# A redrawn order table, five x tiles and four transposed ones, fillers ahead of early waits, and fewer last stores in a fused attention and routed MLP kernel

## The chip, the cores and the metric

The kernel runs on one core of one Trainium2 chip. The metric is the device time of one execution in microseconds; the median of three runs of the kernel before is 752.19 us (751.41 to 753.65). A core has TensorE (PE; PEld is its loading of weights, which overlaps), VectorE (DVE), ScalarE (ACT), GpSimd (POOL) and SyncE (SP, which here only issues transfers), each with its own queue of instructions in program order; they wait for one another by semaphores.

## What is computed

```python
# x: B=8, H=8, S=512, D=64     state: B=8, H=8, Ns=32, D=64
scores = scale * x @ state.T;   a = softmax(scores);    xread = a @ state
scores2 = scale * state @ x.T;  a2 = softmax(scores2);  sread = a2 @ x
t = concat([xread, sread], axis=2)      # 544 tokens per b, laid out as 4352 x 512

logits = t @ w_gate                     # 512 x 8 experts
P = exp(logits - logits.max())
for _ in range(8):                      # Sinkhorn
    P /= P.sum(1, keepdims=True) + 1e-9
    P /= P.sum(0, keepdims=True) + 1e-9
    P *= N / E
out = sum over e of P[:, e:e+1] * (relu(t @ w1[e]) @ w2[e])     # w1[e] 512x1024, w2[e] 1024x512
```

Every token goes through every expert; P only weighs the results.

## The kernel before

The work has two stages. The first holds the attention, the gate, the Sinkhorn loop and expert 0, all mixed; the second holds experts 1 to 7, one block of tokens after the other. There are nine blocks: eight of 512 x tokens (one per b) and one of 256 state tokens (all b together).

The first stage is a list of operations. Each has a number, the engines it may run on, the operations it comes after, and the tiles it takes. `PLAN` is a table written out by hand: each entry is an operation number and a letter for its engine (P TensorE, V VectorE, A ScalarE, G GpSimd, S SyncE's queue, H nothing on the chip). `issue` walks through the table and emits each operation on its engine; so the table sets the order on every engine and, where an operation may run on several, which one runs it. Numbers such as `{"DVE": (0.60, 0.80)}` and the due times beside them are a planner's costs; the emitted code does not read them. Tiles of a pool are handed out in turn (`Ring`, `Slot`): the next one waits until the readers of the tile that had the same place are through.

For each b, the parts of the first stage are:

- two loads of x (`x_nat`, line 468), issued on GpSimd's queue, into one of four tiles of pool `axp`;
- transposed x (`xT`), one of three tiles of pool `axt`: for b 0 and 1 by TensorE (line 578) and copies (`keepX`), for the rest by DMA transposes that SyncE issues (line 591);
- for each half q of the heads, scores on TensorE (`psB`, line 605), and for the first two half-groups also direct scores (`psA`, line 684) that need the spread state `stD`;
- softmax A (x attends to the state): transpose to `eA` (line 628), row maximum (`mxA`, 631), subtraction (`subA`, 648), exponential on ScalarE (656), sums and reciprocals (666, 667), normalization (`normA`, 670, on VectorE or GpSimd), transpose to `aT` (674; for the first two half-groups by TensorE, line 709, and a copy);
- softmax B (the state attends to x): maximum `nmB` (640), bias `nsB` (644), exponential `E` (652), reciprocal `rrec` (659), normalization (`normB`, 662, on VectorE or GpSimd), a DMA transpose to `ETs` that SyncE issues (line 742), and the read `su_ps` (line 758), kept in `xsT` by `keepS`.

The state itself is loaded into `st_st`, cast to `st_in`, transposed by TensorE (line 492) and kept as `stT`. `G_ps` (line 520) is the gate's weight seen through the state; `gate_ps` (788) gives the logits. The Sinkhorn loop (lines 826 to 848) alternates VectorE work with a TensorE matmul by ones (`csb_ps`, line 846) that sums over partitions.

Expert 0: `v_ps` (line 870) projects w1 through the state into `V` (read out by ScalarE or VectorE), `hps` (line 897) is the hidden layer, `hT` its relu, `yps` (line 935) the second layer, kept in `acc`. At the end of the table come expert 1's first projections and hidden block, its sums of weights `T` (`sums_w`, line 965), and then the second stage.

In the second stage `layer2` (line 324 on) forms a block's second product from seven products of 128x256 matmuls (line 334) that accumulate in the banks A, E and two banks `Bseed`; `layer1` (line 255) makes the next block's hidden layer between them, and `project` (line 235) the next projections. Where n is 0, at the very first block, `seed` (line 353) opens each `Bseed` bank with one matmul whose result is overwritten, and `weigh` multiplies expert 0's result by P. `layer2_last` handles the state tokens of the last expert: two rows of 128 tokens, the second in two column halves, each row stored by four transfers of 32 tokens (line 317), two on SyncE's and two on ScalarE's queue.

Of the kernel before, what the change touches and what calls it, by code (L numbers as in the profile page):

```python
# [17 lines left out]
46V 62P 50H 51G 61A 71V 63P 60A 52G 64V 11G 72V 73A 80P 65V 12G 435P 401P 66A 81V 13H 79P 14G 82V 436A 88V  # L18
437A 404P 83A 67V 402A 137H 403A 89V 96H 97P 100P 84V 406A 68V 90A 98A 15G 85V 69P 86P 53G 405A 99V 87V 70A
103P 101A 102A 91V 409P 16H 92G 413P 104V 407P 410A 411P 105V 111A 438P 120P 414V 408A 419P 421P 106V 415P  # L20
112V 138S 121V 74V 439A 412A 422V 113V 417P 107A 54G 440A 75G 122V 432P 429P 123V 370V 420A 469P 128A 418A
416A 17G 108V 140P 124A 125V 423P 426P 471A 433P 114A 148V 93S 129V 430P 149V 172H 424P 76S 434A 115V 470A
109G 130V 139S 110V 126G 141V 131A 427P 18G 127V 142V 428V 431A 445P 143V 132V 94P 150A 95V 77P 425A 156P 116G
447P 151V 133V 78V 449P 446A 443P 441P 144A 455P 164V 152G 448A 117S 19H 450V 157V 444A 165V 173S 442A 451P
456A 166A 134S 20G 452A 453P 463P 158V 472P 207H 145V 175P 159V 183V 184V 457P 31G 146G 454A 176V 473A 160A
464P 185A 174S 460P 458P 461P 465A 147V 161V 21G 153S 177V 191P 47P 162G 474A 118P 167V 459A 154P 462A 178V
163V 135P 49A 168G 199V 22H 48V 179A 466P 136A 352P 475P 200V 192V 201A 193V 119V 467P 476A 194V 23G 195A 485P
202V 208S 210P 180V 169S 155A 218V 356P 353A 481P 357V 468A 487P 219V 24G 489P 181G 186V 211V 242H 486A 482A
477P 490V 488A 483P 479P 220A 170P 478A 503P 187G 480A 484V 171A 203G 196V 537P 209S 25H 212V 226P 197G 504A
505A 506P 213V 500P 182V 198V 26G 234V 221V 507A 222V 204S 188S 491P 27G 538A 227V 539A 501P 497P 502A 508A  # L30
492P 235V 243S 228V 244S 214A 229V 511P 215V 236A 523P 230A 498P 494P 216G 245P 495P 515P 512V 499A 277H 231V
524A 493A 517P 246V 253V 223S 496A 247V 521P 516A 237V 254V 519P 509P 522V 518A 248V 513P 232G 189P 520A 255A
205P 510V 224P 514V 540P 28H 278S 261P 249A 190V 269V 29G 225A 270V 262V 531P 534P 206V 238G 250V 532P 256V
358P 271A 535P 217V 541A 533A 233V 542A 312H 279S 263V 272V 536A 354P 280P 528P 543P 529P 525P 288V 289V 251G
555P 264V 281V 265A 282V 239S 257V 526P 359A 266V 544A 530V 556A 545P 355A 547P 549P 273G 553P 527A 546V 571P
313S 290A 548A 283V 605P 550A 554V 296P 267G 606V 304V 572A 305V 240P 573A 557P 284A 607A 558A 551P 297V 552A
568P 360P 258S 241V 285V 30G 291V 306A 559P 562P 574P 298V 252V 315P 299V 286V 569P 576A 268V 323V 563P 575A
274S 300A 560P 570A 292G 316V 361A 561A 581P 564A 307V 565P 362P 324V 317V 301V 325A 302G 566P 363V 582A 326V
579P 587P 583P 287V 314S 588V 591P 567A 580A 639P 608P 584A 592A 347H 303V 331P 577P 348G 641V 640A 610A 609A
339V 293S 589P 585P 275P 332V 259P 578A 327G 586A 260A 590A 294P 340V 308G 333V 341A 593P 309S 318V 319A 334V  # L40
295V 364P 594P 276V 328S 625P 619P 342V 595A 335A 365A 599P 320V 602P 343V 336V 600P 337V 603P 626A 321G 322V
329P 310P 350G 344S 601A 349G 311A 620V 345P 338V 346V 604V 366P 596P 330A 368P 369V 351G 597P 367A 371V 611P
372P 598A 695H 615P 617P 373V 612V 374P 375V 613P 614V 616A 623P 618A 621P 696H 711H 376A 705P 377V 642P 624A
622A 706A 707A 630P 643V 697V 708P 644A 378P 379V 631P 710A 627P 698V 380V 647P 632A 709A 636P 628P 381P 633P
699V 648V 637P 382V 634P 657P 629A 638A 383V 700V 653P 658A 655P 384P 651P 635A 701V 654A 725P 385V 723P 386V
702V 656A 726A 716P 652A 724A 717A 645P 659P 649P 714P 646A 650A 660A 387P 721P 715A 712P 727P 687P 722A 388V
728A 688A 667P 713A 664P 389V 390P 703V 665P 668P 391V 673P 674A 392V 661P 670P 669A 729V 393P 671P 394V 666A
662P 672A 677P 395V 718P 663A 678A 679P 675P 683P 719A 681P 720V 680A 676A 685P 396P 684A 682A 397V 686A 692P
704V 689P 693P 690P 730P 398V 694A 399P 733P 731V 691A 732A 735A 734A 400V
# [68 lines left out]
def kernel(  # L118
# [63 lines left out]
    outs = out.rearrange("(b s) d -> b s d", s=SB)[:, S:, :]  # L182
# [32 lines left out]
    axp = actx.enter_context(tc.tile_pool(name="attn_x", bufs=4))  # L215
    axt = actx.enter_context(tc.tile_pool(name="attn_xt", bufs=3))
# [46 lines left out]
    def layer1(e, bi):  # L263
# [35 lines left out]
    def layer2_last():  # L299
# [4 lines left out]
        nb = 128 // Ns  # L304
        for row in range(tn // 128):
# [10 lines left out]
            for i in range(nb):  # L316
                (nc.scalar if i % 2 else nc.sync).dma_start(
                    out=outs[row * nb + i], in_=acc[ds(i * Ns, Ns), k, :])

    def layer2(e, bi, n):  # L320
# [30 lines left out]
        def seed(i):  # L351
            bb = bank([128, 2, DH], FP32, "Bseed", "B%d" % i)
            nc.tensor.matmul(bb.rearrange("p c d -> p (c d)"), identh, aT[:, 0, 0], start=True, stop=True)
# [12 lines left out]
        if not n:  # L366
            seed(1)
# [67 lines left out]
    st_in = spl.tile([128, B, NQ, 2, D], FP16, name="st_in")  # L435
    st_st = spl.tile([128, B, NQ, D], FP32, name="st_st")
    loads = []
    for g in range(2):
        def load(g=g):
            bs = ds(g * B // 2, B // 2)  # L440
            (nc.scalar if g else nc.sync).dma_start(
                out=st_st[:, bs], in_=state[bs].rearrange("b (q h) n d -> (h n) b q d", q=NQ))

        loads.append(dma((0, 0), 1.0, load, lands=2.7))
        ops[-1].since, ops[-1].hard = 0.5, 1
# [14 lines left out]
    xn = [slot(axp, 4, [128, H, NSC * D], FP16, "x_nat") for _ in range(B)]  # L460
# [649 lines left out]
```

## Time and profile before

| | us |
|---|---|
| median of three runs | 752.19 |
| the profiled execution | 752.75 |
| its span, first to last instruction | 751.0 |
| TensorE busy | 736.0 |
| VectorE busy | 617.0 |
| ScalarE busy | 517.7 |
| GpSimd busy | 70.8 |

In the span's 40 slices a digit is the busy share in tenths. In a row of stages the columns are the stretch, its length, and then each engine's busy time with its number of instructions, the granted TensorE clock (1.00 is full), the share of the DMA engines and GB/s. In a row of the timeline the first number is the start, the second the length of a run of equal instructions; the bracket gives the idle time ahead of it on its engine and what ended it. In a row of groups stand line, engine, operation, written and read tile, shapes and count, then busy us and mean ns of one, then the idle time before. The end of a matmul is modelled, so two neighbours overlap in the rows; the step from start to start is the better measure of what one costs.

### The profile page before, as it was taken

What the parts mean: (1) busy time and instruction counts of PE and PEld (TensorE: products, weight loads), DVE (VectorE), ACT (ScalarE), POOL (GpSimd) and SP (SyncE); (2) the same over time, 40 slices, a digit from 0 to 9 for tenths busy, and PEclk for the clock granted to TensorE, in tenths of its full rate; (3) what the DMA queues carried; (4) which work ended last, traced back from release to release, by engine and by line L of the source; (5) the groups of instructions that cost most, each with busy time, mean ns of one, the idle gap of its engine ahead of it and who ended that gap; (6) DMA issues with size and microseconds to landing.
All of it is one profiled execution on the core that took longest, in us unless ns stands there. A gap on an engine that the chain in (4) does not pass through costs nothing.

```text
span 751.0 us, 16151 instructions
## 1 busy us (share of the span) xinstructions
PE 736.0 (98%) x6517; PEld 502.2 (67%) x6517; DVE 617.0 (82%) x1529; ACT 517.7 (69%) x1014; POOL 70.8 (9%) x81
## 2 busy tenths in 40 slices
PE   5999999999999999999999999999999999999997
PEld 3444445666777777776776767776777767767776
DVE  5899989877888789788888788887897888887885
ACT  6876856799876766667666766667666676667662
POOL 4674410200010000100000000100001000000000
PEclk9899999999999999999999999999999999999999
DMA  9997560600033000700007000330007000002234
GB/s 179 140 134 131 82 99 1 109 6 1 1 61 53 2 1 2 113 1 2 1 2 112 2 1 1 58 57 1 1 2 112 2 1 2 1 31 94 103 113 141
DMA packets 51323, 36.71 MB, mean 49 GB/s; under 512 B 25392, under 2 KB 43824, under 8 KB 51248
## 3 DMA queue, kind: packets, MB, share of 16 engines
q0 software_dynamic: 22272, 20.97, 18.5%
q1 hardware_dynamic: 27744, 14.18, 7.6%
q8 instruction: 51, 0.84, 0.5%
q10 hardware_dynamic: 1232, 0.52, 0.3%
q14 instruction: 24, 0.20, 0.1%
HBM read 42.48 MB, written 8.91 MB: 68 GB/s over the span
## 4 chain that ended last, share of the span: by engine, by line
PE 92%; DVE 3%; DMA 1%; ACT 1%; POOL 1%; issue 0%; SPq 0%; POOLq 0%; DVEq 0%; ACTq 0%
PE hps L255 28%; PE Bseed L334 20%; PE A L334 14%; PE E L334 14%; PE yps L935 6%; PE hps L897 4%; PE v_ps L235 4%; DMA xT<-x_nat 1%; DMA x_nat<-in_x_dram 1%; PE y L312 0%; PE v_ps L870 0%; POOL a L670 0%; ACT Hm L275 0%; DVE acc L348 0%; POOL E L662 0%; PE su_ps L758 0%
## 5 line engine op out<-in xcount | busy, mean ns | idle before, releaser
L275 ACT ACTIVATE Hm<-hps 128x512 f16<-128x512 f32 (+1 forms) x496 | 265.8, 577 | 130.5 <-PE hps L255 128.1
L255 PE MATMUL hps<-aT,V 128*128 128x512 f16 x880 | 230.6, 379 | 0.0
L334 PEld LDWEIGHTS <-Hm 128*128 128x128 f16 x1888 | 181.6, 98 | 71.3 <-issue 15.9
L348 DVE SCALAR_TENSOR_TENSOR acc<-Bseed,Pmat,acc 128x256 f32<-128x256 f32 x354 | 155.0, 477 | 9.8 <-PE Bseed L334 6.9
L334 PEld LDWEIGHTS <-sm 128*128 128x128 f16 x1416 | 138.3, 98 | 34.5 <-issue 0.3
L334 PE MATMUL A<-w2h,Hm 128*128 128x256 f16 x944 | 123.7, 273 | 0.0
L334 PE MATMUL Bseed<-T,Hm 128*128 128x256 f16 x944 | 123.3, 273 | 0.0
L255 PEld LDWEIGHTS <-V 128*128 128x128 f16 x880 | 86.1, 98 | 50.8
L348 DVE SCALAR_TENSOR_TENSOR acc<-E,Pmat,acc 128x256 f32<-128x256 f32 x236 | 103.2, 476 | 13.8 <-PE E L334 13.5
L281 DVE TENSOR_TENSOR sm<-Hm 128x512 f16<-128x512 f16 (+1 forms) x122 | 50.1, 411 | 60.4 <-ACT Hm L275 60.2
L243 ACT CAST V<-v_ps 128x512 f16<-128x512 f32 x144 | 74.2, 612 | 0.0
L348 DVE SCALAR_TENSOR_TENSOR acc<-A,Pmat,acc 128x256 f32<-128x256 f32 x118 | 51.9, 479 | 17.9 <-PE A L334 17.6
L935 PE MATMUL yps<-w2h,hT 128*128 128x512 f16 x272 | 64.1, 379 | 0.1
L334 PE MATMUL E<-w2h,sm 128*128 128x256 f16 x472 | 61.7, 273 | 0.0
L334 PE MATMUL E<-T,sm 128*128 128x256 f16 x472 | 61.6, 273 | 0.0
L334 PE MATMUL Bseed<-T,sm 128*128 128x256 f16 x472 | 61.5, 272 | 0.0
L363 ACT COPY Bseed<-A 128x512 f32<-128x512 f32 (+1 forms) x62 | 34.1, 550 | 37.9 <-PE A L334 35.3
L282 DVE TENSOR_TENSOR Hm<-Hm 128x512 f16<-128x512 f16 (+1 forms) x122 | 50.3, 412 | 4.2
L284 DVE TENSOR_TENSOR sm<-Hm,sm 128x512 f16<-128x512 f16 (+1 forms) x122 | 50.2, 412 | 4.2
L283 DVE TENSOR_TENSOR sm<-sm,Hm 128x512 f16<-128x512 f16 (+1 forms) x122 | 49.4, 405 | 0.0
L194 POOL DMA_DIRECT2D w1h<-in_moe_w_dram x12 | 8.5, 714 | 396.9 <-PE hps L255 396.5
L935 PEld LDWEIGHTS <-hT 128*128 128x128 f16 x272 | 25.4, 99 | 28.9 <-issue 1.8
(127 smaller groups left out, 617.7 us busy)
## 6 DMA issues: line engine op xcount, KB each, us to landing
w1h<-in_moe_w_dram POOLq DMA_DIRECT2D x16, 512.0 KB, 7.0
w2h<-in_moe_w_dram POOLq DMA_DIRECT2D x16, 512.0 KB, 8.4
out_dram<-acc SPq DMA_DIRECT2D x32, 256.0 KB, 2.5
x_nat<-in_x_dram POOLq DMA_DIRECT2D x16, 256.0 KB, 5.6
st_st<-in_state_dram ACTq DMA_DIRECT2D x1, 256.0 KB, 4.9
st_st<-in_state_dram SPq DMA_DIRECT2D x1, 256.0 KB, 4.2
ETs<-E SPq DMA_TRANSPOSE x16, 4.3
out_dram<-acc SPq DMA_DIRECT2D x4, 64.0 KB, 1.8
```

Source lines behind the costliest of these rows:

```text
L235: nc.tensor.matmul(ps[q][ds(j * Ns, Ns), :], stT[ds(r, 64), bi, q, ds((j ^ q) * Ns, Ns)], w1h[ds(r, 64), 2 * q + j // 2, cols], tile_posit ...
L243: nc.scalar.copy(out=dst, in_=src)
L255: nc.tensor.matmul(out, lhs, rhs, start=(k == 0), stop=(k == len(terms) - 1))
L275: nc.scalar.activation(out=Hm[:, i, j, :tn], in_=hps[:, :tn], func=AF.Relu)
L281: nc.vector.tensor_add(s1, a21, a22)
L282: nc.vector.tensor_sub(a21, a11, a21)
L283: nc.vector.tensor_sub(s2, s1, a11)
L284: nc.vector.tensor_sub(s4, a12, s2)
L334: nc.tensor.matmul(dst[:, c], lhs(j, c), rhs[:, j], start=first and c == 0 and j == 0, stop=(j == NJ - 1), skip_group_check=True)
L348: nc.vector.scalar_tensor_tensor(out=dst, in0=src[:, c], scalar=p[:, k], in1=dst, op0=ALU.mult, op1=ALU.add)
L363: nc.scalar.copy(out=Bb[:, :nk], in_=A[:, :nk])
L935: nc.tensor.matmul(yps.tile, hT[fb].tile[:, ds(tk * 128, 128)], w2h[:, fb, :], start=(fb == 0), stop=(fb == NFB - 1))
```

## The change

- `PLAN` is written anew: other orders on all engines, and other engines for some operations. It has 784 entries (before 736); the Sinkhorn steps are split into single operations so that other work can stand between them, and the sums of weights become single operations that may run on GpSimd.
- The pool of x has five tiles and that of transposed x four. `st_st` and `st_in` no longer have tiles of their own: they are the first tile of these two pools.
- `IDLE` gives operations ahead of which TensorE gets fillers: matmuls of the identity with itself into the tile that the operation then overwrites. Fifty stand ahead of the first transposes of x (operation 56), three ahead of each of the two direct scores (63, 80), eight ahead of a transpose of the second x (97).
- `subA` may run on GpSimd; on GpSimd `normB` is a tensor-tensor product with a broadcast reciprocal instead of a tensor-scalar one.
- The seeds go: the bank of the first `Bseed` is lent to the first `hps` of the second block, which now stands right after the first A product, ahead of the copy of A. `weigh` is done in another order.
- The state tokens of four b are interleaved in `xsT`, so that a row of 128 tokens can be stored by one transfer. The last two rows are stored by three transfers: one for the first row, and one for each half of the second row as soon as that half is done.

In the instruction lists of both kernels, ahead of the second stage: GpSimd runs 12 subtractions (before 0), 10 `normA` (12), 12 `normB` (12) and 6 sums of weights (0); VectorE runs 2 subtractions from `eA` (14), 6 `normA` (4), 4 `normB` (4), 2 sums of weights (8), 5 copies of `xT` (2), 2 of `aT` (1), 4 of `xsT` (9) and 13 of `hT` (16). Ahead of the first `hps` TensorE runs 40 matmuls of `v_ps` (24) and the 64 of `G_ps` (0). On TensorE 6570 matmuls are issued in all: 64 fillers more and two seeds less than before.

```diff
+IDLE = {56: 50, 63: 3, 80: 3, 97: 8}
...
-def issue(ops):
+def issue(ops, idle):
     for step in PLAN:
...
+        idle(op.takes[0].tile if op.takes else None, IDLE.get(int(step[:-1]), 0))
         op.emit(ENGINES[step[-1]])
...
-    outs = out.rearrange("(b s) d -> b s d", s=SB)[:, S:, :]
+    nb = 128 // Ns
+    outs = out.rearrange("(g b s) d -> g s b d", b=nb, s=SB)[:, S:, :, :]
...
-    axp = actx.enter_context(tc.tile_pool(name="attn_x", bufs=4))
-    axt = actx.enter_context(tc.tile_pool(name="attn_xt", bufs=3))
+    axp = actx.enter_context(tc.tile_pool(name="attn_x", bufs=5))
+    axt = actx.enter_context(tc.tile_pool(name="attn_xt", bufs=4))
...
-                hps = bank([128, S], FP32, "hps", "h")
+                if lent is None:
+                    hps = bank([128, S], FP32, "hps", "h")
+                else:
+                    hps, lent = lent, None
...
-            for i in range(nb):
-                (nc.scalar if i % 2 else nc.sync).dma_start(
-                    out=outs[row * nb + i], in_=acc[ds(i * Ns, Ns), k, :])
+                (nc.scalar if c + 1 < parts else nc.sync).dma_start(
+                    out=outs[row, :, :, cols], in_=acc[:, k, cols])
...
-        def seed(i):
-            bb = bank([128, 2, DH], FP32, "Bseed", "B%d" % i)
-            nc.tensor.matmul(bb.rearrange("p c d -> p (c d)"), identh, aT[:, 0, 0], start=True, stop=True)
-            seeds.append(bb)
-
         if not n:
-            for k, eng in enumerate(("DVE", "ACT", "DVE", "POOL")):
+            for k, eng in ((2, "DVE"), (3, "POOL"), (0, "DVE")):
                 weigh(k, eng)
         product(A, h(0, 0), w2h[:, :NJ, :DH], True)
+        Bb = seeds[n % 2]
         if not n:
-            seed(0)
-        Bb = seeds[n % 2]
+            yield
         nc.scalar.copy(out=Bb[:, :nk], in_=A[:, :nk])
+        if not n:
+            weigh(1, "ACT")
         yield
         product(Eb, s(0), T[:, 0], True)
-        if not n:
-            seed(1)
...
-    st_in = spl.tile([128, B, NQ, 2, D], FP16, name="st_in")
-    st_st = spl.tile([128, B, NQ, D], FP32, name="st_st")
+    early = [Slot(rings.setdefault("xT", Ring(4)),
+                  lambda: axt.tile([128, B, NQ, 2, D], FP16, name="st_in", tag="xT")),
+             Slot(rings.setdefault("x_nat", Ring(5)),
+                  lambda: axp.tile([128, B, NQ, D], FP32, name="st_st", tag="x_nat"))]
...
             def normB(eng, E2=E2, rrec=rrec):
-                engines[eng].tensor_scalar(out=E2.tile, in0=E2.tile, scalar1=rrec.tile, scalar2=None,
-                                           op0=ALU.mult)
+                if eng == "POOL":
+                    nc.gpsimd.tensor_mul(E2.tile, E2.tile, rrec.tile.broadcast_to((128, S)))
+                else:
+                    nc.vector.tensor_scalar(out=E2.tile, in0=E2.tile, scalar1=rrec.tile, scalar2=None, op0=ALU.mult)
...
-                s1 = op(r(4), {"DVE": (0.60, 0.80)}, subA, [m1], [], [eA, mxA])
+                s1 = op(r(4), {"DVE": (0.60, 0.80), "POOL": (1.05, 1.20)}, subA, [m1], [], [eA, mxA])
...
-                copy(eng, xsT[:, ds(2 * q, 2), ds(b * Ns, Ns)], su.tile)
+                copy(eng, xsT.rearrange("p c (g n b) -> p c g n b", g=B // nb, b=nb)[:, ds(2 * q, 2), b // nb, :, b % nb], su.tile)
...
-        nc.vector.tensor_sub(T[:, i, jj], p[:, jj], q[:, jj])
+        engines[eng].tensor_sub(T[:, i, jj], p[:, jj], q[:, jj])
...
+    def idle(t, n):
+        if not n:
+            return
+        t = t.rearrange({2: "p a -> p a", 3: "p a b -> p (a b)", 4: "p a b c -> p (a b c)"}[len(t.shape)])[:, :128]
+        for _ in range(n):
+            if t.dtype == FP16:
+                nc.tensor.transpose(t, identh, identh)
+            else:
+                nc.tensor.matmul(t, identh, identh, start=True, stop=True, skip_group_check=True)
+
+    issue(ops, idle)
...
+        if not i:
+            seeds += [bank([128, 2, DH], FP32, "Bseed", "B%d" % k) for k in range(2)]
         l2 = layer2(e, bi, i)
...
+            l1 = layer1(*work[i + 1], None if i else seeds[0].rearrange("p c d -> p (c d)"))
+        if not i:
+            next(l2)
+            next(l1)
```

More of the change, by code (lines that the diff above doesn't have):

```diff
@@ L22 @@
[L22 to L31, printed above, removed]
@@ L442, in load @@
                 out=st_st[:, bs], in_=state[bs].rearrange("b (q h) n d -> (h n) b q d", q=NQ))
-        loads.append(dma((0, 0), 1.0, load, lands=2.7))
+        loads.append(dma((0, 0), 1.0, load, uses=early[1:], lands=2.7))
         ops[-1].since, ops[-1].hard = 0.5, 1
@@ L459 @@
     makeh.since, makeh.hard = 0.7, 1
-    xn = [slot(axp, 4, [128, H, NSC * D], FP16, "x_nat") for _ in range(B)]
+    xn = [slot(axp, 5, [128, H, NSC * D], FP16, "x_nat") for _ in range(B)]
     x_ready = []
@@ L483, in place @@
                 copy(eng, st_in[:, bs, :, s_, :], st_st[:, bs])
-            bd.append(op((0, 0, g), {"DVE": (0.50, 0.64)} if s_ else {"ACT": (0.50, 0.65)}, place, loads[g:g + 1] + warmed))
+            bd.append(op((0, 0, g), {"DVE": (0.50, 0.64)} if s_ else {"ACT": (0.50, 0.65)}, place, loads[g:g + 1] + warmed, uses=early))
     stT_ready = []
@@ L811 @@
     part("ones")
-    op((30.0,), {"DVE": (0.2, 0.3)}, lambda _: nc.vector.memset(ones128, 1.0))
+    ones = op((30.0,), {"DVE": (0.1, 0.25)}, lambda _: nc.vector.memset(ones128, 1.0))
     part("K")
@@ L820 @@
     gb = psum([128, 1], FP32, "gm_ps")
-    c = sk({"PE": (0.18, 0.45)}, lambda: nc.tensor.matmul(gb.tile, ones128[0:1, :], sm_["gm"]), [c], takes=[gb])
+    c = sk({"PE": (0.18, 0.45)}, lambda: nc.tensor.matmul(gb.tile, ones128[0:1, :], sm_["gm"]), [c, ones], takes=[gb])
     c = sk({"DVE": (0.12, 0.25)}, lambda: nc.vector.tensor_copy(out=tile_of("nm", [128, 1]), in_=gb.tile),
@@ L842, in colnorm, with col_rec, col_mul @@
+        def col_rec():
+            nc.vector.reciprocal(out=sm_["crec"], in_=sm_["crec"])
+        def col_mul():
+            nc.vector.scalar_tensor_tensor(out=Pmat, in0=sm_["crec"].unsqueeze(1).broadcast_to((128, NTB, E)),
                                            scalar=float(N) / float(E), in1=Pmat,
                                            op0=ALU.mult, op1=ALU.mult)
-        c = sk({"DVE": (2.10, 2.25)}, rownorm, [c])
+        for emit, us, tail in ((row_sums, 0.43, 0.03), (row_eps, 0.20, 0.03), (row_rec, 0.37, 0.03),
+                               (row_mul, 0.45, 0.03), (col_part, 0.62, 0.15)):
+            c = sk({"DVE": (us, us + tail)}, emit, [c])
```

127 lines of the change are left out of this document (73 added, 54 removed).

## The prediction

> **What bounds the kernel now.** I read the page's busy shares and slices first, then cut the span into stages where TensorE's work changes, then TensorE's timeline in each stage that is not full.
>
> ```profile
> span 751.0 us, 16151 instructions
> PE 736.0 (98%) x6517; PEld 502.2 (67%) x6517; DVE 617.0 (82%) x1529; ACT 517.7 (69%) x1014; POOL 70.8 (9%) x81
> PE   5999999999999999999999999999999999999997
> ```
>
> TensorE (PE) is busy 98% of the span; only the first and the last slice are not full. The stages (us, PE busy, PEld, DVE, ACT, POOL, granted clock, DMA) say what is lost where:
>
> ```profile
> 0.00:6.86 6.86, 0.01 (x1) 0.01 (x1) 1.53 (x4) 2.72 (x4) 6.11 (x14) 1.00 0.87 144
> 6.86:18.86 12.00, 9.86 (x121) 7.03 (x121) 9.29 (x23) 9.15 (x20) 1.40 (x2) 0.88 1.34 199
> 18.86:22.76 3.90, 3.90 (x16) 1.13 (x23) 3.30 (x7) 2.59 (x5) 2.33 (x2) 0.50 1.23 180
> 22.76:135.14 112.38, 110.59 (x1091) 53.47 (x1076) 102.16 (x245) 80.76 (x179) 41.57 (x39) 1.00 0.62 92
> 135.14:743.35 608.21, 608.03 (x5283) 438.30 (x5276) 498.11 (x1248) 422.48 (x808) 19.35 (x25) 1.00 0.17 34
> 743.35:751.00 7.65, 3.63 (x26) 2.25 (x23) 2.60 (x5) 0.00 (x0) 0.00 (x0) 0.92 0.65 206
> ```
>
> The stage of experts 1 to 7, 608.21 us long, idles 0.18 us: nothing but removed TensorE work can shorten it. What the change can win lies ahead of 135.14 (a start of 6.86 us, a thin stretch, 3.90 us at half clock, 1.79 us of waits) and in the tail. The early rows in time (start, length):
>
> ```profile
> 1.00 0.29 POOL masks.py:199 TENSOR_SCALAR_AFFINE_SELECT identh<-identh 128x128 f16<-128x128 f16 x1
> 6.86 1.03 PE L578 MATMUL xT_ps<-identh,x_nat 128*128 128x128 f16 x8 [6.86 <-DMA x_nat<-in_x_dram]
> 9.39 1.06 PE L578 MATMUL xT_ps<-identh,x_nat 128*128 128x128 f16 x8
> 14.63 0.62 PE L578 MATMUL xT_ps<-identh,x_nat 128*128 128x128 f16 x8
> 18.86 3.57 PE L897 MATMUL hps<-aT,V 128*128 128x512 f16 x8
> 22.36 0.58 PE L870 MATMUL v_ps<-w1h,stT 64*32 64x512 f16 x8
> 22.98 1.90 PE L897 MATMUL hps<-aT,V 128*128 128x512 f16 x8
> 26.54 0.41 PE L870 MATMUL v_ps<-w1h,stT 64*32 64x512 f16 x8
> 26.77 0.29 PE L605 MATMUL psB<-xT,stT 64*32 64x256 f16 x8
> ```
>
> Eight equal matmuls take 3.57 us at 18.86 and 1.90 at 22.98: the first dense work falls into the half-clock stretch. The same eight transposes take 1.03 and 1.06 us early and 0.62 at 14.63, so TensorE is slow at the very start as well.
>
> **The change, part by part.** The sum is made on the profiled execution, 752.75 us (its span is 751.0), which lies 0.56 above the median of the runs, 752.19.
>
> *Start of the dense stretch.* Fifty transposes of the identity go ahead of the first x transpose. The identity is there at 1.29; at the slow pitch ((9.39 - 6.86) / 24 transposes = 0.105 us) they last 5.3 us, to 6.6, just before x lands at 6.86. They cost nothing while x is late; at 0.11 each they would end at 6.8. If they leave the array fast, the 12 transposes ahead of the first stT copy (8 of x, 4 of state) finish 12 x (0.105 - 0.052) = 0.6 us sooner (half the pitch at full clock). VectorE waits for exactly that:
>
> ```profile
> 8.35 0.42 DVE L421 COPY stT<-stT_ps 128x512 f16<-128x512 f16 x1 [2.06 <-PE stT_ps L492]
> 10.87 0.69 DVE L640 TENSOR_REDUCE nmB<-psB 128x1 f32<-128x512 f32 x1 [0.48 <-PE psB L605]
> 18.48 0.42 DVE L421 COPY aT<-aT_ps 128x512 f16<-128x512 f16 x1 [0.19 <-PE aT_ps L709]
> ```
>
> From nmB on VectorE is a closed chain up to the aT copy, after which the first hps can start (18.86). With the later transposes faster too, I let nmB start 0.9 us sooner (0.6, and 0.3 of the 0.48). But in the new order VectorE makes one more xT copy and one more aT copy ahead of hps, 0.42 each by these rows; with the 0.19 us wait ahead of aT taken up, 0.6 in all. Net gain 0.3; bounds -0.6 (no faster array) and +0.9 (the copies fit into waits).
>
> *Clock.* The 3 + 3 + 8 further fillers and the G_ps projection are put into the gaps between 11 and 16 us. If the clock holds, the first hps group saves 3.57 - 1.90 = 1.67 and v_ps 0.58 - 0.41 = 0.17: gain 1.85, bounds 0 and 1.85. I take the upper end because TensorE then has work in nearly every microsecond from 1.3 on; no row shows it, which is why its failure is the first rival. A rule of the Trainium skill speaks against this part: TensorE: Matmul & The Clock Gate, section Part 4: PE-mode transpose, says that transposes do not count as TensorE activity for the gate, and 58 of the 64 fillers write fp16 tiles and so are transposes. The trace cannot refute it: after 2.5 us of nothing but transposes, the eight at 9.39 are as slow as the eight at 6.86. By it the sum lacks 1.85 + 0.9 = 2.75.
>
> *Work moved ahead of the dense stretch.* G_ps stood at 42.56 and two more sets of v_ps (40 matmuls instead of 24 ahead of hps) stood in dense work.
>
> ```profile
> 42.56 0.72 PE L520 MATMUL G_ps<-wgh,stT 64*32 64x8 f16 x64
> 43.20 1.12 PE L758 MATMUL su_ps<-ETs,x_nat 128*64 128x32 f16 x48
> ```
>
> By start-to-start times G_ps is 0.64 and a v_ps set 26.77 - 26.54 = 0.23, so 0.64 + 0.46 = 1.1 us leaves the dense stretch. It is hidden under the VectorE chain, where TensorE has 12.00 - 9.86 = 2.1 us free; without that cover the gain is 0. ScalarE pays: ahead of the first hT it now casts 10 V halves for 6, copies sB once and G twice, and loses three xT copies and one aT copy.
>
> ```profile
> L419 ACT CAST V<-v_ps 128x512 f16<-128x512 f32 x36 | 19.9, 603 | 2.7 <-PE v_ps L870 1.9 <-PE psB L605 0.8
> L419 ACT COPY xT<-xT_ps 128x512 f16<-128x512 f16 x6 | 3.4, 623 | 2.3 <-PE xT_ps L578 2.3
> L419 ACT CAST xsT<-su_ps 128x64 f16<-128x64 f32 x7 | 1.5, 226 | 0.9 <-PE su_ps L758 0.9
> ```
>
> Five casts (sB as one) at 0.60 less four copies at 0.62, and 0.4 for the two G (64 elements a partition, as xsT): 3.0 - 2.5 + 0.4 = 0.9 us later for the first relu, behind which the PSUM banks of the following hps and the first yps wait. I charge all of it: -0.9, bounds 0 and -0.9.
>
> *Five x tiles, four transposed ones.* In the stage 22.76 to 135.14 the two waits that name a transfer are for transposed x:
>
> ```profile
> 52.82 0.30 PE L605 MATMUL psB<-xT,stT 64*32 64x256 f16 x8 [0.90 <-DMA xT<-x_nat]
> 60.80 0.30 PE L605 MATMUL psB<-xT,stT 64*32 64x256 f16 x8 [0.45 <-DMA xT<-x_nat]
> ```
>
> The state borrows one tile of each pool and gives it back before x needs it, so x 4 and transposed x 3 wait for no reader. I count 0.90 + 0.45 = 1.35 as gone, bounds 0 and the stage's whole idle time, 112.38 - 110.59 = 1.79. What keeps this true is supply: TensorE comes to each row sooner, so the softmax chains must too. The instruction lists give VectorE 12 subtractions and 6 weight sums less, POOL more:
>
> ```profile
> L648 DVE TENSOR_TENSOR eA<-eA,mxA 128x512 f32<-128x512 f32 x14 | 10.4, 746 | 0.1
> L965 DVE TENSOR_TENSOR T<-w2h 128x512 f16<-128x512 f16 x4 | 1.7, 418 | 0.0
> L662 POOL TENSOR_SCALAR E<-E,rrec 128x512 f16<-128x512 f16 x12 | 19.2, 1600 | 19.5 <-DVE rrec L659 15.3 <-ACT hT L425 4.0
> L670 POOL TENSOR_TENSOR a<-eA,rA 128x512 f16<-128x512 f32 x12 | 12.8, 1066 | 21.6 <-DVE rA L667 12.9 <-DVE logits L421 4.2 <-ACT logits L419 2.4
> L296 POOL TENSOR_SCALAR acc<-acc,Pmat 128x512 f32<-128x512 f32 x1 | 1.8, 1846 | 38.5 <-DVE Pmat L841 38.5
> ```
>
> VectorE is relieved of 12 x 0.746 + 6 x 0.418 = 11.5 us. POOL's normalization of E changes from a tensor-scalar (1.60) to a tensor-tensor, for which the nearest row is 1.07. The subtraction on POOL lies between 1.07 and 1.85 (float32 out); I take 1.07, whose operation it shares. POOL's softmax work goes from 19.2 + 12.8 = 32.0 to 12 x 1.07 + 10 x 1.07 + 12 x 1.07 = 36.4 us, up to 45.7. The x loads and, through E, SyncE's transposes are queued behind it. VectorE's relief (9 us before the routing) covers an arrival some 4 us earlier. The routing's first matmul now stands further ahead of the end of the stage, and the weight sums follow POOL's last loads: both off the path. Queued triggers and small casts get no term.
>
> *Seeds.* Two matmuls that only opened the accumulation banks go; the lent bank takes an hps that was due anyway.
>
> ```profile
> 136.03 0.38 PE L353 MATMUL Bseed<-aT,identh 128*128 128x512 f16 x1
> 136.41 1.03 PE L334 MATMUL E<-T,sm 128*128 128x256 f16 x8
> 137.28 0.38 PE L353 MATMUL Bseed<-aT,identh 128*128 128x512 f16 x1
> 137.49 0.59 PE L255 MATMUL hps<-aT,V 128*128 128x512 f16 x2
> ```
>
> (136.41 - 136.03) + (137.49 - 137.28) = 0.59 gained; at least 0.4 (two of the smaller).
>
> *Tail.* After the last VectorE product four stores are issued, two on each queue; now one of 128 KB.
>
> ```profile
> 747.02 0.48 DVE acc L314
> L317 SPq DMA_DIRECT2D out_dram<-acc x4: 314/380/420, 746.1 to 747.9; - x4
> L317 ACTq DMA_DIRECT2D out_dram<-acc x4: 375/406/433, 746.1 to 748.0; - x4
> ```
>
> One issue of about 0.4 us falls away behind 747.50; shorter rows may land slower. I take 0.3, bounds -0.3 and 0.5.
>
> Sum: 0.3 + 1.85 + 1.1 - 0.9 + 1.35 + 0.59 + 0.3 = 4.6. The profiled time becomes 752.75 - 4.6 = 748.15, the median 752.19 - 4.6 = **747.6 us**.
>
> **The rivals.**
> *The clock is lost all the same.* For it: the slow transposes at 9.39. Against it: the added work between 11 and 16. The 1.85 goes and the start is -0.6 for 0.3: 4.6 - 2.75 leaves 1.85, 750.3 us. This is also the case in which the fillers do not do what the change says. The skill's rule for transposes leads here.
>
> *The waits only move.* For it: VectorE is busy 102.16 of 112.38 us. Against it: the 11.5 us taken off it. TensorE then stands at the same supply later, and 1.1 and 1.35 fall away: gain 2.15, 750.0 us.
>
> *POOL becomes the bound (slower).* If the subtraction costs 1.85 instead of VectorE's 0.75, each of 12 chains is 1.1 us longer, and loads and normalizations queue behind it. With 0.7 us of each exposed on TensorE: 12 x 0.7 - 4.6 = 3.8 us slower, 756.0. It decides from 4.6 / 12 = 0.4 us exposed each. Against it: POOL would be busy 45.7 of some 70 us.
>
> **How the numbers follow.** Chances: forecast 0.61, clock lost 0.19, waits move 0.10, POOL 0.10. No change that this measurement can tell is within 0.3%, 2.26 us, so faster means under 749.9. Of the forecast nearly all (0.59), of clock lost and waits move under half (0.13 of 0.29) lie there: faster 0.72, same 0.18, slower 0.10. The best bounds (start 0.9, no charge on ScalarE, idle 1.79, tail 0.5) add 2.1: 745.5. The range runs from there to 751.0, over both middle cases, and leaves POOL out.
>
> **What would show it.** Right: a granted clock of 1.0 through 15 to 23 us, first hps near 18.5 with eight matmuls in 1.9 us, no psB waiting for xT, the first A product near 131.4 (135.14 less the first five terms), POOL's subtraction near 1.07 us. Wrong: a 0.50 row over the first hps, new waits of TensorE on a or eA from POOL, or a first A product later than 133.

## The result and the profile after

| | before | after |
|---|---|---|
| median | 752.62 us (22 runs, 751.41 to 754.26) | 751.87 us (22 runs, 747.03 to 754.20) |
| ratio | 1 | 0.9979, 95% interval 0.9969 to 0.9989 |
| profiled execution | 752.75 | 749.25 |
| its span | 751.0 | 747.5 |

The median falls by 0.75 us, which is less than the 0.3% that the prediction called the least that can be told from no change, though over 22 runs the interval stays below 1. The prediction had 747.6 and a range of 745.5 to 751.0: the sign is right, the size is six times too large, and the time lies outside the range. The two profiled executions differ by 3.5 us. So the profile below is of one of the better executions of a kernel whose times now spread over 7 us (before: 3 us here, 3.1 to 4.6 us in the later groups of runs), and the question is what the others lose.

The stages of the profile after, cut at TensorE's own marks (stretch, length, busy time with instructions of PE, PEld, DVE, ACT, POOL, granted clock, DMA share, GB/s):

```profile
0.00:6.66 6.66, 5.15 (x50) 4.98 (x51) 1.75 (x4) 2.72 (x4) 5.92 (x13) 1.00 0.89 146
6.66:12.86 6.20, 4.63 (x122) 3.50 (x123) 5.17 (x13) 4.59 (x10) 1.60 (x3) 0.99 1.26 199
12.86:19.76 6.90, 5.85 (x113) 3.96 (x95) 4.94 (x15) 4.97 (x13) 0.00 (x0) 0.51 1.40 200
19.76:22.95 3.19, 3.19 (x30) 1.35 (x30) 3.15 (x8) 3.19 (x8) 2.54 (x3) 1.00 1.20 164
22.95:132.10 109.15, 107.72 (x1006) 52.55 (x1006) 93.92 (x227) 78.60 (x176) 52.06 (x54) 1.00 0.66 94
739.90:747.50 7.60, 3.66 (x26) 2.27 (x24) 2.59 (x5) 0.00 (x0) 0.00 (x0) 0.94 0.57 207
```

The half-clock stretch is still there, but it now lies from 12.86 to 19.7, in the thin stretch ahead of the first `hps`, and in this execution the first dense work behind it runs at full clock. TensorE's timeline to the first dense work (start, length, then in the bracket the wait ahead and who ended it):

```profile
1.35 5.15 PE L1049 MATMUL xT_ps<-identh 128*128 128x128 f16 x50 [1.35 <-POOL identh masks.py:199]
6.66 0.62 PE L585 MATMUL xT_ps<-identh,x_nat 128*128 128x128 f16 x8 [0.17 <-DMA x_nat<-in_x_dram]
...
10.66 0.63 PE L893 MATMUL v_ps<-w1h,stT 64*32 64x512 f16 x16 [0.34 <-DMA w1h<-in_moe_w_dram]
11.64 0.30 PE L612 MATMUL psB<-xT,stT 64*32 64x256 f16 x8 [0.36 <-ACT E L659]
...
12.64 0.63 PE L527 MATMUL G_ps<-wgh,stT 64*32 64x8 f16 x63 [0.69 <-ACT V L420]
14.31 0.63 PE L893 MATMUL v_ps<-w1h,stT 64*32 64x512 f16 x8 [1.05 <-DMA w1h<-in_moe_w_dram]
...
19.76 3.19 PE L920 MATMUL hps<-aT,V 128*128 128x512 f16 x14
```

The first eight transposes take 0.62 us (before: 1.03), and TensorE reaches its first `v_ps` at 10.66 (before: 12.15). Four waits for the load of w1, for E and for V then take 2.4 us (before, five waits take 2.1). Behind the last of them, from 14.31 on, TensorE waits for nothing; its thin work runs at a granted clock of 0.51 for 5.45 us. The first `hps` comes 0.90 us later than before, at 19.76. Then comes a stretch that has no counterpart before:

```profile
35.94 0.43 PE L767 MATMUL su_ps<-ETs,x_nat 128*64 128x32 f16 x16
37.14 0.68 PE L767 MATMUL su_ps<-ETs,x_nat 128*64 128x32 f16 x32 [0.77 <-DMA ETs<-E]
37.75 2.76 PE L958 MATMUL yps<-w2h,hT 128*128 128x512 f16 x12
40.45 0.41 PE L893 MATMUL v_ps<-w1h,stT 64*32 64x512 f16 x8
41.06 0.30 PE L612 MATMUL psB<-xT,stT 64*32 64x256 f16 x8 [0.21 <-DMA xT<-x_nat]
```

The wait for transposed x has shrunk to 0.21, but a read of `su_ps` stands 0.77 us for its transposed E. The end of the first stage and the step from there to the end of the span, first TensorE's timeline after, then one row of stages each, after and before:

```profile
132.10 1.05 PE L340 MATMUL A<-w2h,Hm 128*128 128x256 f16 x8
132.99 0.59 PE L260 MATMUL Bseed<-aT,V 128*128 128x512 f16 x2
133.63 1.03 PE L340 MATMUL E<-T,sm 128*128 128x256 f16 x8
134.50 0.59 PE L260 MATMUL hps<-aT,V 128*128 128x512 f16 x2
134.94 1.04 PE L340 MATMUL Bseed<-T,sm 128*128 128x256 f16 x8
```

```profile
132.10:747.50 615.40, 611.23 (x5304) 440.50 (x5296) 500.39 (x1251) 423.02 (x809) 19.36 (x25) 1.00 0.17 36
```

```profile
135.14:751.00 615.86, 611.66 (x5306) 440.56 (x5298) 500.71 (x1253) 422.48 (x808) 19.35 (x25) 1.00 0.17 36
```

From the first A product to the end there are 615.40 us after and 615.86 before. In the profiles of the thirteen runs below that keep this second stage the same difference of span and first A lies between 615.3 and 615.4. In these profiles all that varies is therefore when the first A starts, and each is summed up by that one number.

### The profile page after: what moved, and what is told of

It reads as the page before. It is cut to its first block, busy times and chain, and to the rows that moved or that the text cites. A ratio compares the mean times of both kernels' runs of the same rounds, so it can differ in the third digit from the quotient of the medians.

```text
span 747.5 us, 16270 instructions
## 1 busy us (share of the span) xinstructions
PE 737.8 (99%) x6579; PEld 506.8 (68%) x6579; DVE 609.3 (82%) x1513; ACT 517.1 (69%) x1014; POOL 81.5 (11%) x97
## 3 DMA queue, kind: packets, MB, share of 16 engines
q1 hardware_dynamic: 27840, 14.31, 7.9%
## 4 chain that ended last, share of the span: by engine, by line
PE 92%; DMA 2%; DVE 2%; ACT 2%; POOL 1%; issue 0%; SPq 0%; POOLq 0%; ACTq 0%
PE hps L260 28%; PE Bseed L340 20%; PE A L340 14%; PE E L340 14%; PE yps L958 6%; PE v_ps L240 4%; PE hps L920 3%; DMA w1h<-in_moe_w_dram 1%; DMA xT<-x_nat 1%; ACT hT L426 1%; PE v_ps L893 1%; PE y L319 0%; DVE acc L354 0%; ACT Hm L283 0%; PE su_ps L767 0%; ACT V L420 0%
```

## The experiments

The first four runs set a theory Gate (the gain stands and falls with the granted clock) against a theory Supply (TensorE is fed by loads, transposes and VectorE, and what it gains it waits for). Each median stands beside that of the kernel before on the same chip in the same group of runs, which was 752.5 to 753.0 throughout.

**The same kernel again**

> The changed kernel once more, for a second trace. Two theories. Gate: the granted clock is decided in stretches of 3.41 us from how busy TensorE was in the stretch before; the new order still leaves TensorE waiting between 10 and 16 us, so the clock falls to half again, and the time depends on where that stretch falls against the first hps. Supply: the time is set by what TensorE waits for (w1h, V, the softmax chain), whatever the clock, and the spread has another cause. Gate expects another place or length of the half-clock stretch in this trace, and the span moved with it (745.3 with none, near 747.5 with one of 6.8 us ahead of hps, 750 and more when it lies over hps). Supply expects the same waits and a first hps at 19.8 again.

Measured: 751.82 us (12 runs), ratio 0.9983, interval 0.9967 to 0.9999. The profile (span 750.7) is of an ordinary execution, 752.48 us. TensorE's timeline:

```profile
35.07 0.43 PE L767 MATMUL su_ps<-ETs,x_nat 128*64 128x32 f16 x16
39.08 0.68 PE L767 MATMUL su_ps<-ETs,x_nat 128*64 128x32 f16 x32 [3.58 <-DMA ETs<-E]
39.69 4.45 PE L958 MATMUL yps<-w2h,hT 128*128 128x512 f16 x12
...
135.32 1.05 PE L340 MATMUL A<-w2h,Hm 128*128 128x256 f16 x8
```

```profile
39.70:44.10 4.40, 4.40 (x23) 1.54 (x22) 0.00 (x0) 1.65 (x6) 0.88 (x2) 0.61 0.84 119
```

The same read waits 3.58 us instead of 0.77, the granted clock in the 4.4 us behind it is 0.61, and the twelve `yps` take 4.45 us instead of 2.76. Wait and slow clock together, 3.58 - 0.77 + 4.45 - 2.76 = 4.5 us, are more than the whole difference of the first A between the two executions (135.32 - 132.10 = 3.2), and the first A of this one comes 0.18 us later than before the change. Neither theory foresaw this: a half-clock stretch did lie elsewhere, as Gate said, but behind a wait for this read, which neither names, and Supply's first `hps` near 19.8 came at 18.95.

The mean granted clock is on record for every execution. Among the 34 of the changed kernel, the 8 with 0.997 or more have a median of 748.1 us (747.0 to 750.3), the 26 with 0.995 or less one of 752.0 (749.3 to 754.4). The clock goes with the time, then; what the executions without a profile waited for is not shown.

**No fillers, and more of them**

```diff
-IDLE = {56: 50, 63: 3, 80: 3, 97: 8}
+IDLE = {}                                            # e1_no_fillers
+IDLE = {56: 50, 63: 6, 80: 8, 483: 6, 449: 8, 486: 16, 97: 8, 452: 4, 100: 4, 86: 8, 103: 6}   # e2_filled
+SPARE = {47: 14}                                     # e2_filled
```

`SPARE` gives fillers behind an operation, here fourteen behind 47 into the unused part of its bank.

> The changed kernel without its 64 fillers. Gate: the transposes at 6.9 us run at half speed (about 1.03 us for eight), VectorE's chain starts about 1.3 us later, and a half-clock stretch lies over the first hps as in the kernel before: 1 to 2 us slower than the change, near 753, spread no wider than before's 3 us. Supply: within 0.5 us of the change.

> The changed kernel with 71 more fillers in its waits between 8.8 and 18 us (ahead of both direct scores, five v_ps sets, G_ps, both transposes of the second x, an aT transpose and a score). Gate: no half-clock row between 6 us and the tail, first hps near 17.7, first A product near 130, span near 745.4 and time near 747.1, with a spread under 2 us. Supply: the first hps stays near 19.8 and the median within 0.7 us of the change's 751.9.

Measured: without fillers 751.0 us (ratio 0.9977, 0.9968 to 0.9986), with more of them 751.31 us (0.9984, 0.9971 to 0.9998). The edit adds 74 fillers, not the 71 of the expectation. Neither can be told from the changed kernel, and Gate's expectation is missed both ways: in the second profile the clock is 1.00 throughout, and the first A comes at 135.14 all the same. Supply has the second kernel's median, but the first one lies 0.8 us under the changed kernel, where it allowed 0.5. Both have the wait; first the kernel without fillers, then the filled one:

```profile
38.85 0.88 PE L767 MATMUL su_ps<-ETs,x_nat 128*64 128x32 f16 x32 [1.85 <-DMA ETs<-E]
39.66 4.16 PE L958 MATMUL yps<-w2h,hT 128*128 128x512 f16 x12
```

```profile
39.74 0.68 PE L769 MATMUL su_ps<-ETs,x_nat 128*64 128x32 f16 x32 [1.25 <-DMA ETs<-E]
40.36 2.76 PE L960 MATMUL yps<-w2h,hT 128*128 128x512 f16 x12
```

What TensorE gains or loses at the start disappears in a wait that a transfer ends.

**The fillers in the kernel before**

The order table of before with the four groups of fillers of the change.

> The kernel before with the change's four groups of fillers and nothing else. Gate: the first transposes run fast and VectorE's chain starts about 1.5 us sooner, but the waits behind it are as long as before, so the clock falls again over the first hps: 0 to 1.5 us faster than before, with the change's wide spread. Supply: the same as before within 0.5 us.

Measured: 753.90 us (11 runs), ratio 1.0016, interval 1.0007 to 1.0025. Alone, the fillers make the old order a little slower, by 1.35 us; Gate had 0 to 1.5 us faster and Supply the same within 0.5, so both missed. Its profile shows new waits of 2.69 us for w1 at 15.03 and of 1.77 us of `su_ps` for ETs at 51.22.

From here on the theory under test is called Read: the time is lost where a read stands in TensorE's order ahead of the landing of its transposed E.

**One read later, one read sooner**

```diff
 # e4_read_later: the read of the third tile's first half-group and its eviction
-118P 154P 500V 94P 505P ... 155A 119A 208S 178G 551P 179A 161V 191P 512P 162G 553A ... 525P 507A
+118P 500V 94P 505P ... 119A 208S 178G 551P 179A 161V 191P 154P 512P 162G 553A 155A ... 507A 525P
 # e5_read_sooner
-499P 145V 159G 489P 174S 501P 497P 175P 492A 504A 490A 160A 118P 154P ... 155A
+499P 154P 145V 159G 489P 174S 501P 492A 497P 175P 504A 490A 160A 155A 118P
```

> The changed kernel with one read moved: the sixteen su_ps matmuls of the third x tile's first four heads (154P) stand behind the next 12 yps, 8 v_ps and 8 psB instead of ahead of them, some 3.4 us of matmuls later; its eviction (155A) moves with it, and 507A goes ahead of 525P. Theory Read (the time is lost where this read stands before its transposed E has landed, 0.77 to 3.58 us in four profiles, plus up to 1.7 us of cold clock in the yps behind it): no wait of su_ps for ETs over 0.3 us between 30 and 45 us, the clock at 1.00 in 35 to 50 us, the first A product at 130.5 to 132.5, median 748.0 to 749.5. Rival Supply (the attention stage takes what the loads and VectorE's chain of scores give, and a wait taken away returns as another): waits of the same sum under other names before 60 us, A near 134 to 135, median 751 to 752.

> The same read moved the other way: it stands ahead of the last three hps of the second tile, of 8 psB and of the 16 su_ps of the second tile, some 2.0 us of matmuls sooner than in the changed kernel (155A and 492A move with it). Theory Read: the wait grows by those 2.0 us (2.8 to 5.6 us), median 753.0 to 754.5. Rival Supply: the work that is put behind the wait fills what would have been waits later, median 751.5 to 752.5.

Measured: later, 748.52 us (5 runs, 747.89 to 750.42), ratio 0.9950, interval 0.9934 to 0.9966; sooner, 754.25 us (12 runs), ratio 1.0018, interval 1.0003 to 1.0034. Both medians lie in Read's ranges and outside Supply's. Some 2.0 us of matmuls sooner cost 754.25 - 751.82 = 2.4 us; some 3.4 us later give 3.3. The profile of the read sooner:

```profile
39.72 0.62 PE L767 MATMUL su_ps<-ETs,x_nat 128*64 128x32 f16 x16 [5.29 <-DMA ETs<-E]
40.27 2.74 PE L920 MATMUL hps<-aT,V 128*128 128x512 f16 x6
```

In the profile of the read later no `su_ps` waits. The next in line shows instead: eight `psB` wait 1.10 us for transposed x at 41.86. That part of Supply is true, but it is a third of the 3.58 us above. The profile is of the slowest of the five executions; fourteen `hps` at 19.97 take 4.17 us, partly at half clock, and the first A starts at 133.26, later than the 132.5 expected and 2.1 us ahead of the ordinary execution of the changed kernel.

**The same two kernels again, with and without fillers**

`e7_read_later_no_fillers` and `e10_no_fillers_again` are `e4_read_later` with `IDLE = {}`; `e9_read_later_again` is `e4_read_later` unchanged.

> e4_read_later without the filler matmuls (IDLE empty). Theory Read: within 0.5 us of e4_read_later, since taking the fillers away alone gave 751.0 against 751.8. If a full clock at the first hps is worth its price once the later wait is gone (the prediction's step of 1.85 us): 1.0 to 2.0 us above e4_read_later, with hps at 0.40 us a piece for 3 to 7 us after 19 us.

> e4_read_later, the same kernel again, for its median: 748.0 to 749.5 if the first result holds; over 750.5 if it was luck of five runs.

> e7_read_later_no_fillers, the same kernel again. If the fillers are worth the prediction's 1.85 us once the wait is gone: 1.5 to 3.5 us above e9_read_later_again, mean clock 0.995 (two windows of 3.41 us at half speed) against 0.997. If the first difference (3.3 us) was chance: within 0.7 us of it.

Measured: 751.81 us (12 runs; ratio 0.9985, 0.9972 to 0.9999) without fillers against 748.52 with; again 751.43 us (12 runs; 0.9985, 0.9974 to 0.9996) against 747.69 (6 runs; 0.9939, 0.9926 to 0.9953). So the changed kernel with the read moved has 748.1 as the mean of two medians (the second a little under the 748.0 that was expected), and it beats both kernels. The fillers, worth nothing while the wait stood, are worth 3.3 and 3.7 us without it, against the 0.5 that Read allowed, the 1.85 of the prediction and the 3.5 that was the most expected of the second pair. The same four numbers say something against Read: without fillers, moving the read gains nothing (751.81 and 751.43, against 751.0 for `e1_no_fillers`). There the waits do only move: the read's 1.85 us is gone, and `psB` waits 2.58 and 2.85 us for transposed x instead. The fillers and the moved read pay together, and neither pays alone. The profiles of the second pair, with fillers first:

```profile
19.30 3.19 PE L920 MATMUL hps<-aT,V 128*128 128x512 f16 x14
...
40.89 0.30 PE L612 MATMUL psB<-xT,stT 64*32 64x256 f16 x8 [0.96 <-DMA xT<-x_nat]
...
132.29 1.05 PE L340 MATMUL A<-w2h,Hm 128*128 128x256 f16 x8
```

```profile
19.25 3.73 PE L920 MATMUL hps<-aT,V 128*128 128x512 f16 x14
...
42.45 0.30 PE L612 MATMUL psB<-xT,stT 64*32 64x256 f16 x8 [2.85 <-DMA xT<-x_nat]
...
134.19 1.05 PE L340 MATMUL A<-w2h,Hm 128*128 128x256 f16 x8
```

Of the 1.9 us between these two executions 0.54 is the slower `hps`; the longer wait for transposed x is 1.89, of which TensorE's earlier arrival takes a part. That transpose of x lands 9.0 us after its issue without fillers and 6.7 us with them (8.7 and 6.8 in the first pair), and the transpose of E issued just ahead of it the other way round, after 4.1 and 7.5 (4.3 and 5.7). Why the two share the time differently is not shown; the fillers' worth is measured, its way through the transfers stays open.

**The subtractions back on VectorE**

```diff
 # e6_subtract_on_vector: the twelve subA entries of the table, such as
-123G 143G 159G 178G 194G 213G
+123V 143V 159V 178V 194V 213V
```

> The changed kernel with its 12 subtractions of L655 back on VectorE (0.69 us each there, 1.04 on POOL; VectorE 8.3 us busier between 25 and 90 us). If moving them was worth what the prediction assumed for VectorE's relief (nothing of its own), 751 to 752.3; theory Supply, with VectorE's chain of scores as what sets the pace: 753 to 755, with TensorE waiting for VectorE's results; theory Read: no change beyond 0.5 us, the same wait for ETs at 36 to 40 us.

Measured: 754.32 us (8 runs), ratio 1.0028, interval 1.0010 to 1.0045; the first A comes at 136.83, behind waits of 1.71 us for transposed x at 32.48 and of 1.14 us for a relu on ScalarE at 51.08. This is in Supply's range (753 to 755) and against Read, which allowed 0.5 us. The twelve subtractions are worth 2.5 us where the change put them, though each is dearer there (1.10 us on GpSimd against 0.69 on VectorE). That VectorE's queue then holds TensorE up is argued, not shown: the two waits name a transfer and ScalarE.

**Scores later too, and full clock on top**

```diff
 # e8_read_and_scores_later (on e4)
-551P 179A 161V 191P 154P 512P
+551P 154P 179A 161V 512P 191P
 # e11_later_and_filled: e8 with IDLE and SPARE of e2_filled
```

> e4_read_later with the next thing in line moved too: the 8 psB of the fourth tile's second four heads (191P), which stood 1.10 us for their transposed x in e4_read_later and 2.58 us in e7_read_later_no_fillers at 42 us, go behind 4 more yps (0.9 us), and the read 154P ahead of them. Theory Read, widened (each read or score placed ahead of its DMA transpose costs its wait, and the first one moved away shows the next): no wait over 0.5 us between 30 and 45 us, first A 0.3 to 1.1 us before that of e4_read_later, median 747.0 to 748.5. Rival Supply: VectorE gets the scores later and TensorE waits for its results (aT, V) before 60 us, median 748.5 to 750.

> e8_read_and_scores_later with the 71 further filler matmuls of e2_filled, which kept the clock full but brought the first hps 0.9 us later. Theory Gate (the clock is what is left): clock 1.00, median 746 to 747.5, 1 us below e8. Rival: the fillers cost at the start what the clock saves: the first hps after 20 us, median 748 to 749.5.

Measured: 749.56 us (12 runs; 0.9963, 0.9950 to 0.9976) and 751.52 us (12 runs; 0.9986, 0.9974 to 0.9998). Putting the scores later removes their wait: between 30 and 45 us no transfer is waited for over 0.2 us, and the first A, at 132.59, is 0.67 ahead of that of `e4_read_later`, as Read said; it is 0.30 behind that of `e9_read_later_again`, though, which is the same kernel as `e4_read_later`, so this shows little. And the median is 1.5 us above that of `e4_read_later` and `e9_read_later_again`, in the range of Supply, which has VectorE get the scores later: at 45.64 the next `psB` waits 0.39 us for VectorE in the one profile there is, a quarter of the difference. The fillers that keep the clock at 0.998 to 1.0 in all twelve executions cost more than they save, and by more than the rival's range: the first `hps` comes at 20.36, the first A at 134.29.

**The loads of x out of the way**

```diff
 # e12_x_loads_later (on the changed kernel), e13_both_later (on e4)
-144A 20G 78A 165V 496A 21G 166A ... 207H 498V 511P 146G 133G
+144A 78A 165V 496A 166A ... 498V 511P 146G 20G 21G 207H 133G
```

> The changed kernel with the two 256 KB loads of the fifth x tile (20G, 21G, with the host step 207H) issued after POOL's next two subtractions and a normalisation, some 4 us later than before, so that the transpose of E (153S, issued at 32.1 to 32.5 us) has them no longer beside it; the read 154P stays where it is. If the loads make the transpose late: it lands 2.5 to 4 us after its issue instead of 4.9 to 6.7, the wait of su_ps falls under 0.7 us, median 748.5 to 750.5. If the transpose takes that long by itself or behind older transfers: landing after 4.5 to 7 us as before, the same wait, median 751 to 752.5.

> e4_read_later with the same two loads later. If the loads beside the transposes set the landings: the psB wait of 1 us for the transposed x at 41 us shrinks too, median 747 to 748.5, no slower than e4_read_later; otherwise the fifth tile comes later and its scores wait, 748.5 to 750.

Measured: 749.71 us (12 runs; 0.9969, 0.9955 to 0.9982) and 750.67 us (8 runs; 0.9973, 0.9961 to 0.9984). The transpose in question (the one issued nearest to 32 us), its landing and the read behind it:

| | issued at | lands after | read starts at | waited |
|---|---|---|---|---|
| after | 32.11 | 4.9 | 37.14 | 0.77 |
| e0, the same kernel | 32.22 | 6.7 | 39.08 | 3.58 |
| e1, no fillers | 32.53 | 6.2 | 38.85 | 1.85 |
| e5, read sooner | 33.17 | 6.4 | 39.72 | 5.29 |
| e12, loads later | 31.41 | 3.2 | behind the first two reads, in order | none |

Issue and landing add up to the start of the read, within 0.2 us, in each of the four that wait. In the twelve profiles in which the two 256 KB loads of x are issued beside it, this transpose lands after 4.1 to 7.5 us. In the two with the loads at 35.7 and 36.2 it lands after 3.2 and 2.4, and in `e12_x_loads_later` all 48 `su_ps` run on end:

```profile
35.28 1.19 PE L767 MATMUL su_ps<-ETs,x_nat 128*64 128x32 f16 x48
36.40 2.76 PE L958 MATMUL yps<-w2h,hT 128*128 128x512 f16 x12
...
43.45 0.43 PE L767 MATMUL su_ps<-ETs,x_nat 128*64 128x32 f16 x16 [0.71 <-DMA ETs<-E]
```

So the loads of x beside it make the transpose late, and its landing, after 4.9 and 6.7 us, is what the two profiled executions of the changed kernel differ by. Not all of the spread is that: the runs of `e12_x_loads_later` still lie 3.9 us apart. The last row of the profile is the price of the edit: GpSimd issues the loads ahead of the next normalization of E, whose transpose is then late for its own read. On top of the moved read the edit makes things worse: 750.67, above both ranges expected (747 to 748.5, or 748.5 to 750) and 2.5 us above the moved read alone. The wait for transposed x is gone from its profile, and two waits of 0.60 us, for a transposed E at 43.90 and for ScalarE at 45.27, have come; whether these are the 2.5 us is not shown.

## Why the prediction was wrong

*The step that failed* is the one on the five x tiles and four transposed ones: "I count 0.90 + 0.45 = 1.35 as gone, bounds 0 and the stage's whole idle time". The two waits did go (0.21 is left). But the bounds only asked how much of the old waits could vanish; they left no room for a new one, and so the sum counted as a gain what the new table spends elsewhere. The prediction even quoted the row that carries the danger, 48 `su_ps` at 43.20, and used it only as the end of `G_ps`. Among these 48 is the read of the third tile's first half-group, sixteen matmuls in, at 43.6; its transpose was issued at 38.45 and landed 4.6 us later, at 43.05, 0.5 us ahead of it. After the change the transpose is issued at 32.11, 6.3 us sooner, but TensorE is at the read by 36.37, 7.2 us sooner, and two loads of x are issued beside the transpose where there was one. It lands at 37.0 in the better profile, at 38.9 in an ordinary one. The rival "the waits only move" named the mechanism in general and priced it at 750.0; the price was too low, because behind the waits of 1.85, 3.58 and 5.29 us for the read the clock also fell to half: 0.77 us lost in the better profile, 3.58 + 1.69 = 5.3 in an ordinary one. With the read moved out of this wait, the two medians lie 4.4 and 4.8 us under those of the kernel before, about the 4.6 that was forecast. That the sum then comes out is in part luck, since its terms do not hold one by one, as follows. No run takes the added tiles away, so what they alone are worth stays open.

*Start of the dense stretch* (+0.3 taken, bounds -0.6 to 0.9): -0.90, outside its bounds. VectorE's `nmB` did come sooner, even more than said (9.24 against 10.87), but the first `hps` did not follow: `v_ps` at 14.31 waits for w1's second part, and behind it TensorE's own thin work takes 5.45 us at a granted clock of 0.51. The step took VectorE for the limit; here VectorE's last copy of `aT` itself waits 0.69 us for TensorE's transposes. The load of w1 alone does not set the start either. In `e0_change_again` TensorE does not wait for it, and the first `hps` still comes at 18.95; in `e12_x_loads_later` the same work behind a later load (14.59) takes 4.39 us at a clock of 0.67, and the first `hps` comes at 18.98.

*Clock* (+1.85): the size was there in the profiled execution, 14 `hps` in 3.19 us, that is 8 in 1.8, but by luck. The clock did not hold, as the step assumed; the sign of being right was a clock of 1.0 from 15 to 23 us, and it was 0.51 up to 19.7. The half-clock stretch only ended just ahead of the first `hps`, and its price went into the start. With the same fillers the 14 `hps` take 3.19 us in one profile of the moved read and 4.17 in the other, and without any they take 3.18 in `e1_no_fillers`. The rule on transposes that the prediction weighed against it (the Trainium skill, TensorE: Matmul & The Clock Gate, Part 4: PE-mode transpose) is refuted here: TensorE did nothing but fifty transposes from 1.35 to 6.5, and the eight behind them took 0.62 us, against 1.03 where nothing ran ahead (the kernel before, and the kernel without fillers). What the fillers are worth in the median is not the 1.85 either: nothing as long as the wait for ETs stood, 3.3 to 3.7 us without it.

*Work moved ahead* (+1.1) and *ScalarE's charge* (-0.9) are not told apart by any run. Together with the clock, the waits and the start they make 135.14 - 132.10 = 3.04 us on the first A of the profiled execution, where the first five terms said 3.7.

*GpSimd*: its subtraction measured 1.10 us on average, 1.07 was taken, and no wait of TensorE behind the first fillers names it. The rival that it becomes the bound is refuted by its reverse: taking the subtractions off GpSimd costs 2.5 us. The prediction gave VectorE's relief no term of its own; it should have had one.

*Seeds and tail* (0.59 and 0.3): together 615.86 - 615.40 = 0.46. From the start of the last VectorE product to the end of the span there are 3.98 us before and 3.90 after, so the tail gives 0.1, under what was taken, and the seeds 0.4: the E product waits 0.2 us behind the lent `hps` (0.64 from start to start, where two such matmuls take 0.44 from 134.50 to 134.94), the rest is as worked out.

The sum was made on one execution, and for that one it is not far off: 4.6 said, 3.5 measured, with the start 1.2 us worse than its term. The median is not that execution's: a sum on one profile says nothing of a wait that this execution happened to keep short, and the changed kernel's executions spread over 7 us where those before spread over 3.

## What to carry to other kernels

When an order is tightened, list every consumer that moves forward and set its new place against issue plus landing of the transfer that feeds it, with the slowest landing the trace shows and not the median; and ask what else is issued beside that transfer. Measure the parts of a change on a version without the wait that hides them: the fillers were worth nothing beside it and over 3 us once it was gone, and moving the wait was worth nothing without the fillers.

## What the runs showed of the hardware

A transpose of E by DMA, issued near 32 us, lands 2.4 and 3.2 us after its issue with the loads of x kept away and after 4.1 to 7.5 us with two of them beside it, in nearly the same program; one kernel shows 4.9 and 6.7 in two executions. A transpose of x, twice the size, takes up to 9.0 us there.

Behind a wait of 1.85 us among thin matmuls (32 moving columns) the clock fell to half: in the kernel without fillers the stretch from 39 to 42 us has a granted clock of 0.52.

```profile
38.00:39.00 1.00, 0.15 (x10) 0.18 (x11) 1.00 (x4) 0.28 (x1) 0.00 (x0) 1.00 1.12 237
39.00:42.00 3.00, 3.00 (x38) 1.50 (x34) 1.49 (x4) 1.65 (x6) 2.78 (x3) 0.52 0.90 95
```

The Trainium skill (TensorE: Matmul & The Clock Gate, section Why this matters for your kernels) advises against idle gaps over about 3 us; here the clock fell behind a shorter one in that execution, while it stayed at 1.00 behind the 1.25 us of the filled kernel, and also behind the 2.58 and 2.85 us that `psB` waits in the two profiles with the read moved and no fillers. The length of one wait alone does not decide it.
